# Running sums kept in PSUM, a shorter norm and casts moved to ScalarE, in an attention and two-MLP kernel

## Chip, cores and metric

The kernel runs on one core of a Trainium2 chip. The metric is the device time of one execution in microseconds (us). TensorE is called PE, VectorE DVE, ScalarE ACT, GpSimd POOL; SyncE (SP) issues the DMA transfers.

## The reference

```python
kv  = einsum('bhsd,bhse->bhde', k, v)          # linear attention, 8 batches x 8 heads, 576 x 64
out = einsum('bhsd,bhde->bhse', q, kv)
x   = out / sqrt(mean(out*out, -1) + 1e-6) * g_norm   # -> 4608 tokens x 512
h   = x @ w_in                                 # 512 -> 2048      (MLP one)
g   = maximum(h, 0) + log1p(exp(-abs(h)))      # softplus
x   = g @ w_out                                # 2048 -> 512
h   = maximum(maximum(x @ w1, x @ w2), x @ w3) # 512 -> 768       (MLP two)
y   = h @ w_out2                               # 768 -> 512
```

Everything is fp32, and all three projections of MLP one and two use the same tokens.

## The kernel before

The 4608 tokens are taken in five passes of 928, 928, 928, 928 and 896, each as two halves of N = 464 (448) columns. A matrix product over two halves of tokens and two halves of features is done by a scheme with seven block products instead of eight (`ORDER`: 1, 5, 6, 2, 7, 4, 3). One such set of seven is a *group*. The left factors are sums of weight blocks, the right factors sums of token blocks (`combine`). Pass 0 multiplies in plain fp32 and meanwhile converts the weights from 8-byte words (`to_f32`, `sums_of_weights`), splits each into a high and a low part (`make_unit`) and stores them to DRAM. Passes 1 to 4 load these units (`u`) and replace a product by three (high x high, high x low, low x high: `mm3`, lines 123 to 125). `split` makes the parts of a token block: a cast gives `hi` (line 107 on ACT, line 109 on DVE), then a subtraction gives `lo` (line 113, on POOL or DVE).

A pass has 16 groups for MLP one (H0 to H7 from x to h, X00 to X31 from g back to x), 9 groups for MLP two (three feature blocks f, and j = 0, 1, 2 for w1, w2, w3), and the output products. All work is written as events with a due time in *slots*; one slot is one product, a group begins every 7 slots, and groups overlap: `SLOT` puts a group's products at 0, 1, 3, 4, 6, 9, 12 slots after its beginning. Events are sorted by due time, and a scheduler that goes by its own estimates of durations fixes each engine's order when the kernel is built, so the order on an engine can differ from the written one.

The products accumulate in PSUM banks by tag: X (2 buffers; products 1, 6, 7, 4), Y (2; products 5, 3), W (1; product 2), `at` (2; attention and parts of the output), `cv` (1). `sums` takes the four result blocks out: C11 = X + W, C12 = X + Y, C22 = X + Y, C21 = X. ACT copies X to an SBUF tile, DVE adds the other bank to that tile, and the tile goes to `done`. For H groups `done` is `softplus`: ACT takes Abs, Exp and Ln (lines 346 to 348), DVE max(h, 0) + e (line 349). For MLP two it is the running maximum (line 617), and after j = 2 a split into `hh` and `hl`. W is also the bank of a temporary, t2, in `combine`.

`attention_beside` puts the next pass's attention into MLP two: eight head steps (two halves by four pairs of heads), 6 slots apart. A step at slot t loads q at t - 6, splits it at t - 3 (`split_q`: cast on DVE, low part on POOL), multiplies with kv at t + 0.3 (`out_mm`), squares and splits at t + 0.4 (`square`: Square on ACT, cast sh on DVE, low part sl on POOL, og = o * g on ACT), sums the squares with two matmuls against ones at t + 3.3 (`ssq_mm`, lines 465 and 466) and normalises at t + 3.4 (`norm`). `combine_x` takes the results at the end of the pass. All units u, the q and the k and v tiles are loaded by the one queue of SP.

At the border from X31 to MLP two, `combine_x2(q)` splits the two feature halves q = 0, 1 of x; the first group of MLP two cannot finish product 1 before the parts of q = 1 are there.

Of the kernel before, what the change touches and what calls it, by code (L numbers as in the profile page):

```python
# [7 lines left out]
F32 = mybir.dt.float32  # L8
# [7 lines left out]
P = 128  # L16
# [21 lines left out]
def kernel(  # L38
# [57 lines left out]
    gcol = const.tile([P, 1], F32, name="gcol")  # L96
    ones = const.tile([P, P], F32R, name="ones")
# [109 lines left out]
    def convert(g, i):  # L207
        if i == 0:
            sw[g] = pools["raw"].tile([P, 8, 256], F32, tag="sw", bufs=3, name="sw")
        w = sw[g]  # L210
        if i == 0:
            dst = w[:, PLACE[1]:PLACE[2] + 1:PLACE[2] - PLACE[1]]
        else:
            dst = w[:, PLACE[4]:8:7 - PLACE[4]]
        to_f32(raws.pop((g, i)), dst)

    def sums_of_weights(g):
        w = sw[g]
        a11, s1, s2, a12, s3, a22, s4 = (w[:, PLACE[m]] for m in (1, 5, 6, 2, 7, 4, 3))
        a21 = w[:, 7]  # L220
        add(nc.gpsimd, s1, a21, a22)
        sub(nc.gpsimd, s2, s1, a11)
        sub(nc.gpsimd, s3, a11, a21)
        sub(nc.gpsimd, s4, a12, s2)
# [31 lines left out]
    def combine(tile, dst, c, tiles, steps, t2_bank):  # L256


        b11, b12, b21, b22 = tiles
        n = b11.shape[1]  # L260
        for s in steps:
            for m in STEPS[s]:
                hi, lo = tile("hi", n, F32R), tile("lo", n, F32R)
                src = {1: b11, 2: b21, 3: b22, 7: b12, 4: b11}.get(m)
                if m == 5:
                    src = t1 = psum("cv", "t1")[:, 0:n]
                    sub(nc.vector, t1, b12, b11)
                elif m == 6:
                    src = t2 = psum(t2_bank, "t2")[:, 0:n]
                    sub(nc.vector, t2, b22, t1)  # L270
                    sub(nc.gpsimd, b12, b22, b12)
                    sub(nc.vector, b11, b21, t2)
                split(nc.scalar, src, hi, lo, nc.vector if m in (5, 6) else nc.gpsimd)
                dst[m, c] = (hi, lo)
# [42 lines left out]
    def sums(done, make):  # L317

        c = {}

        def after(m, b):
            if m == 1:
                c[11] = make(11)
                nc.scalar.copy(c[11], b["X"])
            elif m == 6:
                c[12] = make(12)
                nc.scalar.copy(c[12], b["X"])  # L327
            elif m == 2:
                add(nc.vector, c[11], c[11], b["W"])
                done(11, c[11])  # L330
            elif m == 7:
                c[22] = make(22)
                nc.scalar.copy(c[22], b["X"])
                add(nc.vector, c[22], c[22], b["Y"])
                done(22, c[22])
            elif m == 4:
                done(21, b["X"])
            elif m == 3:
                add(nc.vector, c[12], c[12], b["Y"])
                done(12, c[12])  # L340

        return after
# [73 lines left out]
    def split_q(a, n, p):  # L416
        q = q_t.pop((a, p))
        qh, ql = ctile("qh", n, F32R), ctile("ql", n, F32R)
        split(nc.vector, q, qh, ql, nc.gpsimd)
        qs[a, p] = (qh, ql)  # L420
# [30 lines left out]
    def square(a, n, p):  # L451
# [4 lines left out]
        split(nc.vector, sq, sh, sl, nc.gpsimd)  # L456
# [12 lines left out]
    def norm(a, n, p):  # L469

        ss = ss_t.pop((a, p))
        m, r, t = ctile("m", n), ctile("r", n), ctile("t", n)
        nc.vector.tensor_scalar(
            out=m, in0=ss, scalar1=1.0 / D, scalar2=EPS, op0=ALU.mult, op1=ALU.add
        )
        nc.scalar.activation(r, m, AF.Ln)
        nc.scalar.activation(r, r, AF.Exp, scale=-0.5)
        nc.scalar.activation(t, r, AF.Square)
        nc.vector.scalar_tensor_tensor(
            out=t, in0=t, scalar=-0.5, in1=m, op0=ALU.mult, op1=ALU.mult  # L480
        )
        nc.vector.scalar_tensor_tensor(  # L482
            out=r, in0=t, scalar=1.5, in1=r, op0=ALU.add, op1=ALU.mult
# [22 lines left out]
    def attention_beside(pas, t_kv, t0):  # L506
# [11 lines left out]
        for k in range(2 * NP):  # L518
# [7 lines left out]
            at(t + 3.3, ssq_mm, a, n, p)  # L526
            at(t + 3.4, norm, a, n, p)

    def run_pass(pas, base):
# [31 lines left out]
        for fp in range(8):  # L561
            t = start[f"H{fp}"]
            weights_at(t, G_H[fp])
            run_group(t, pas, G_H[fp], R,
                      sums(lambda w, src, fp=fp: h_done(fp, w, src), lambda w: ctile(f"h{w}", N)))
# [30 lines left out]
        def combine_x2(q):  # L596
            tiles = [x2[q, w] for w in TILES]
            if pas == 0:
                combine32(xc_tile, R2, q, tiles)
            else:  # L600
                combine(xc_tile, R2, q, tiles, ALL, "W")
# [26 lines left out]
        for k in range(9):  # L628
# [5 lines left out]
                           lambda w, j=j: ge_tile(pas, f"m{w}", N) if j == 0 else ctile(f"m{w}", N)))  # L634
# [61 lines left out]
    for j in range(2):  # L696
        r = slice(j * D, (j + 1) * D)
        nc.gpsimd.memset(ones[r, r].bitcast(F32), 1.0)
        nc.gpsimd.memset(ones32[r, r], 1.0)
    nc.sync.dma_start(out=gcol, in_=gn)  # L700

# [44 lines left out]
def _laid_out(inputs):  # L746
# [15 lines left out]
    def swapped(w):  # L762

        w = w.reshape(-1, 2, P, 2, DM // 2)
        w = np.stack([w[:, 0], w[:, 1, :, ::-1]], axis=1)
        return np.ascontiguousarray(w).reshape(-1, P, DM)

# [13 lines left out]
        "w_in": swapped(cols(inputs["moe_w_in"])),  # L781
        "w_out": swapped(wo.reshape(NF, P, DM)),
        "w123": np.ascontiguousarray(
            np.stack([swapped(cols(inputs[f"moe2_w{j}"])) for j in (1, 2, 3)], axis=1)
# [28 lines left out]
```

## Time and profile before

| | before |
|---|---|
| median of 3 runs (range) | 1546.93 us (1544.9 to 1549.52) |
| profiled execution: time, span | 1547.21 us, 1545.3 us |
| mean granted PE clock | 0.981 |
| busy share of span: PE, DVE, ACT, POOL | 94%, 63%, 52%, 50% |
| busy us: PE, DVE, ACT, POOL | 1447.1, 976.7, 805.7, 778.9 |
| DMA moved, mean rate | 315.58 MB, 204 GB/s |

The span runs from the first to the last instruction. Pass 0 ends at about 440 us; each later pass takes about 275 us. A row of a windows view gives, after the window, its length and then for PE, PE's weight loads, DVE, ACT and POOL the busy us with the number of instructions in brackets, then the granted PE clock as a share of full speed, the DMA share and GB/s. In a timeline a row gives start, length, engine, line, operation, output<-inputs, and in square brackets the idle time of the engine just before and what ended it.

### The profile page before, as it was taken

To read this page: it belongs to the slowest core of one execution; us is meant where nothing else is said; L and a number is where in the kernel's file an instruction comes from. 1 tells how busy PE (TensorE), PEld (TensorE's weight loads), DVE (VectorE), ACT (ScalarE), POOL (GpSimd) and SP (SyncE) were. 2 spreads that over 40 slices of the span, in tenths; PEclk is the share of its full clock that TensorE was granted. 3 is DMA by queue.
4 is the path that set the end of the run, shared out by engine and by line. 5 is a ranking of instruction groups with operands and counts; after the bars stand their busy time and mean duration, and the time that the engine had idled before them with its cause. 6 is when DMAs were issued, how large, how long until landed. Compare 5 with 4: busy or idle time off the path is not lost.

```text
span 1545.3 us, 18956 instructions
## 1 busy us (share of the span) xinstructions
PE 1447.1 (94%) x6164; PEld 1136.4 (74%) x6164; DVE 976.7 (63%) x1495; ACT 805.7 (52%) x1573; POOL 778.9 (50%) x692
## 2 busy tenths in 40 slices
PE   6699999888999998999999899999998999999898
PEld 4244444444478887888888788888887889898798
DVE  6687897768836665771766566456765753667332
ACT  4486552545448653553866344377635445774321
POOL 4668676867606444552435544534446551534311
PEclk9799999999999999999999999999999999999999
DMA  7547668665566676655567675566665656666563
GB/s 258 213 162 249 223 223 292 229 231 175 201 209 195 202 246 188 201 178 185 190 204 217 215 241 180 162 207 194 222 207 171 195 181 189 202 211 214 176 213 115
DMA packets 106803, 315.58 MB, mean 204 GB/s; under 512 B 11984, under 2 KB 22224, under 8 KB 106704
## 3 DMA queue, kind: packets, MB, share of 16 engines
q1 hardware_dynamic: 106704, 314.36, 62.2%
q8 instruction: 50, 0.82, 0.2%
q14 instruction: 49, 0.40, 0.1%
HBM read 255.85 MB, written 58.46 MB: 203 GB/s over the span
## 4 chain that ended last, share of the span: by engine, by line
PE 60%; ACT 12%; DVE 11%; POOL 8%; issue 4%; DMA 4%; SPq 0%; POOLq 0%; ACTq 0%; DVEq 0%
PE Xo L124 3%; PE Xo L125 3%; PE Xo L123 3%; PE Xx L123 3%; PE Xx L124 3%; PE Xx L125 3%; PE Xh L123 3%; PE Xh L125 3%; PE Xh L124 3%; DMA v<-in_vp_dram 2%; PE oacc L652 2%; PE oacc L124 2%; PE oacc L125 2%; PE oacc L123 2%; ACT hi L107 2%
## 5 line engine op out<-in xcount | busy, mean ns | idle before, releaser
L113 POOL TENSOR_TENSOR lo<-e,hi 128x464 fp32r<-128x464 f32 (+1 forms) x160 | 195.9, 1257 | 223.6 <-ACT hi L107 220.0
L349 DVE SCALAR_TENSOR_TENSOR e<-h,e 128x464 f32<-128x464 f32 (+1 forms) x120 | 113.8, 949 | 75.7 <-ACT e L348 75.4
L119 POOL TENSOR_TENSOR e<-e 128x464 f32<-128x464 f32 (+1 forms) x40 | 48.4, 1209 | 161.2 <-DVE t L119 147.0
L113 POOL TENSOR_TENSOR u<-sw,u 128x512 fp32r<-128x512 f32 (+1 forms) x100 | 119.5, 1221 | 11.5 <-ACT u L107 11.5
L124 PE MATMUL Xo<-lo,u 128*128 128x464 f32 (+1 forms) x288 | 109.4, 380 | 12.5 <-POOL lo L113 12.5
L123 PE MATMUL Xo<-hi,u 128*128 128x464 f32 (+1 forms) x288 | 108.3, 381 | 6.9 <-DMA u<-wd 5.6
L125 PE MATMUL Xo<-hi,u 128*128 128x464 f32 (+1 forms) x288 | 108.1, 378 | 0.0
L113 POOL TENSOR_TENSOR hl<-m,hh 128x464 fp32r<-128x464 f32 (+1 forms) x48 | 59.7, 1249 | 93.0 <-ACT hh L107 88.3
L346 ACT ACTIVATE e<-h 128x464 f32<-128x464 f32 (+1 forms) x120 | 70.3, 586 | 62.0 <-DVE h L116 62.0
L107 ACT CAST hi<-t 128x464 fp32r<-128x464 f32 (+1 forms) x96 | 52.2, 544 | 96.3 <-DVE t L119 39.4
L116 DVE TENSOR_TENSOR x<-x,Xx 128x464 f32<-128x464 f32 (+1 forms) x120 | 75.5, 629 | 41.5 <-PE Xx L125 34.2
L123 PE MATMUL Xh<-hi,u 128*128 128x464 f32 (+1 forms) x256 | 96.7, 378 | 3.7 <-ACT h L327 2.1
L123 PE MATMUL Xx<-hi,u 128*128 128x464 f32 (+1 forms) x256 | 95.5, 373 | 1.9 <-ACT x L582 1.9
L125 PE MATMUL Xx<-hi,u 128*128 128x464 f32 (+1 forms) x256 | 95.0, 371 | 0.0
L125 PE MATMUL Xh<-hi,u 128*128 128x464 f32 (+1 forms) x256 | 94.9, 371 | 0.0
L124 PE MATMUL Xx<-lo,u 128*128 128x464 f32 (+1 forms) x256 | 94.8, 370 | 0.0
L124 PE MATMUL Xh<-lo,u 128*128 128x464 f32 (+1 forms) x256 | 94.6, 370 | 0.0
L107 ACT CAST hi<-e 128x464 fp32r<-128x464 f32 (+1 forms) x160 | 87.4, 574 | 13.0 <-PE Yx L124 7.1
L347 ACT ACTIVATE e<-e 128x464 f32<-128x464 f32 (+1 forms) x160 | 92.7, 588 | 2.2
L348 ACT ACTIVATE e<-e 128x464 f32<-128x464 f32 (+1 forms) x160 | 92.5, 586 | 2.4
L486 POOL TENSOR_TENSOR og<-og,r 128x464 f32<-128x464 f32 (+1 forms) x40 | 52.2, 1306 | 64.7 <-DVE r L482 64.7
L187 ACT ACTIVATE cv<-raw 128x512 f32<-128x512 f32 x56 | 35.9, 640 | 85.0 <-DVE sw L198 44.5
(180 smaller groups left out, 4147.2 us busy)
## 6 DMA issues: line engine op xcount, KB each, us to landing
u<-wd SPq DMA_DIRECT2D x316, 512.0 KB, 4.2
wd<-u SPq DMA_DIRECT2D x79, 512.0 KB, 2.9
u<-wd SPq DMA_DIRECT2D x116, 256.0 KB, 3.7
raw<-in_w_out_dram SPq DMA_DIRECT2D x22, 512.0 KB, 4.3
k<-in_kp_dram SPq DMA_DIRECT2D x32, 320.0 KB, 4.1
v<-in_vp_dram SPq DMA_DIRECT2D x32, 320.0 KB, 4.4
raw<-in_w_dram SPq DMA_DIRECT2D x18, 512.0 KB, 3.6
raw<-in_w_in_dram SPq DMA_DIRECT2D x16, 512.0 KB, 4.2
```

Source lines behind the costliest of these rows:

```text
L107: nc.scalar.copy(hi, src)
L113: eng_lo.tensor_tensor(out=lo, in0=src, in1=hi.bitcast(F32), op=ALU.subtract)
L116: eng.tensor_tensor(out=o, in0=a, in1=b, op=ALU.add)
L119: eng.tensor_tensor(out=o, in0=a, in1=b, op=ALU.subtract)
L123: nc.tensor.matmul(acc, wh, xh, start=first, stop=False, skip_group_check=on)
L124: nc.tensor.matmul(acc, wh, xl, start=False, stop=False, skip_group_check=on)
L125: nc.tensor.matmul(acc, wl, xh, start=False, stop=last, skip_group_check=on)
L346: nc.scalar.activation(e, src, AF.Abs)
L347: nc.scalar.activation(e, e, AF.Exp, scale=-1.0)
L348: nc.scalar.activation(e, e, AF.Ln, bias=1.0)
L349: nc.vector.scalar_tensor_tensor(out=e, in0=src, scalar=0.0, in1=e, op0=ALU.max, op1=ALU.add)
L486: nc.gpsimd.tensor_tensor(out=og, in0=og, in1=r, op=ALU.mult)
```

## The change

- `sums`: C11 of every H group is added in place in bank W and not in the SBUF tile; softplus reads it there. In MLP two with j = 1, 2, C11 and C12 are added in place in W and Y and the maximum reads them there.
- `split_q` and `square`: the casts qh and sh go from DVE to ACT.
- `norm`: the tile m = ss/64 + eps and its DVE instruction are gone. Ln reads ss from PSUM with scale 1/64 and a bias column; the correction step reads ss from PSUM too, and g_norm is multiplied by -0.5 once at the start to make up for the other constants.
- `ssq_mm` and `norm` of each head step are due 1.5 slots later.
- `combine_x2(1)`: the low parts for products 1 and 2 are made on DVE and not on POOL.
- The weight block a21 lies in the place of sum s1, which is then formed in place: the `sw` tile has seven columns of blocks and not eight, s3 is formed ahead of s1, and the host no longer swaps blocks.

```diff
--- before.py
+++ after.py
@@ -94,6 +94,7 @@
         return gc_tile(name, n) if p == 0 else wide(pools["ge"], "ge", 17, name, n)
 
     gcol = const.tile([P, 1], F32, name="gcol")
+    epsc = const.tile([P, 1], F32, name="epsc")
     ones = const.tile([P, P], F32R, name="ones")
     ones32 = const.tile([P, P], F32, name="ones32")
     kvs = []
@@ -206,21 +207,20 @@
 
     def convert(g, i):
         if i == 0:
-            sw[g] = pools["raw"].tile([P, 8, 256], F32, tag="sw", bufs=3, name="sw")
+            sw[g] = pools["raw"].tile([P, 7, 256], F32, tag="sw", bufs=3, name="sw")
         w = sw[g]
         if i == 0:
             dst = w[:, PLACE[1]:PLACE[2] + 1:PLACE[2] - PLACE[1]]
         else:
-            dst = w[:, PLACE[4]:8:7 - PLACE[4]]
+            dst = w[:, PLACE[5]:PLACE[4] + 1:PLACE[4] - PLACE[5]]
         to_f32(raws.pop((g, i)), dst)
 
     def sums_of_weights(g):
         w = sw[g]
         a11, s1, s2, a12, s3, a22, s4 = (w[:, PLACE[m]] for m in (1, 5, 6, 2, 7, 4, 3))
-        a21 = w[:, 7]
-        add(nc.gpsimd, s1, a21, a22)
+        sub(nc.gpsimd, s3, a11, s1)
+        add(nc.gpsimd, s1, s1, a22)
         sub(nc.gpsimd, s2, s1, a11)
-        sub(nc.gpsimd, s3, a11, a21)
         sub(nc.gpsimd, s4, a12, s2)
 
     def make_unit(g, k):
@@ -253,7 +253,7 @@
     STEPS = ((1,), (5, 6), (2,), (7,), (4,), (3,))
     ALL = (0, 1, 2, 3, 4, 5)
 
-    def combine(tile, dst, c, tiles, steps, t2_bank):
+    def combine(tile, dst, c, tiles, steps, t2_bank, on_dve=()):
 
 
         b11, b12, b21, b22 = tiles
@@ -270,7 +270,7 @@
                     sub(nc.vector, t2, b22, t1)
                     sub(nc.gpsimd, b12, b22, b12)
                     sub(nc.vector, b11, b21, t2)
-                split(nc.scalar, src, hi, lo, nc.vector if m in (5, 6) else nc.gpsimd)
+                split(nc.scalar, src, hi, lo, nc.vector if m in (5, 6, *on_dve) else nc.gpsimd)
                 dst[m, c] = (hi, lo)
 
     def combine32(tile, dst, c, tiles):
@@ -316,28 +316,33 @@
 
     def sums(done, make):
 
+
         c = {}
+
+        def total(w, bank):
+            tile, kept = c.pop(w)
+            to = tile if kept else bank
+            add(nc.vector, to, tile, bank)
+            done(w, to)
+
+        def copy(w, b):
+            c[w] = make(w)
+            nc.scalar.copy(c[w][0], b["X"])
 
         def after(m, b):
             if m == 1:
-                c[11] = make(11)
-                nc.scalar.copy(c[11], b["X"])
+                copy(11, b)
             elif m == 6:
-                c[12] = make(12)
-                nc.scalar.copy(c[12], b["X"])
+                copy(12, b)
             elif m == 2:
-                add(nc.vector, c[11], c[11], b["W"])
-                done(11, c[11])
+                total(11, b["W"])
             elif m == 7:
-                c[22] = make(22)
-                nc.scalar.copy(c[22], b["X"])
-                add(nc.vector, c[22], c[22], b["Y"])
-                done(22, c[22])
+                copy(22, b)
+                total(22, b["Y"])
             elif m == 4:
                 done(21, b["X"])
             elif m == 3:
-                add(nc.vector, c[12], c[12], b["Y"])
-                done(12, c[12])
+                total(12, b["Y"])
 
         return after
 
@@ -416,7 +421,7 @@
     def split_q(a, n, p):
         q = q_t.pop((a, p))
         qh, ql = ctile("qh", n, F32R), ctile("ql", n, F32R)
-        split(nc.vector, q, qh, ql, nc.gpsimd)
+        split(nc.scalar, q, qh, ql, nc.gpsimd)
         qs[a, p] = (qh, ql)
 
     def out_mm32(a, n, p, tag):
@@ -453,7 +458,7 @@
         sq = ctile("sq", n)
         sh, sl = ctile("sh", n, F32R), ctile("sl", n, F32R)
         nc.scalar.activation(sq, o, AF.Square)
-        split(nc.vector, sq, sh, sl, nc.gpsimd)
+        split(nc.scalar, sq, sh, sl, nc.gpsimd)
         og = xr_tile(1, "og", n)
         nc.scalar.mul(og, o, gcol)
         sq_t[a, p] = (sh, sl)
@@ -469,18 +474,15 @@
     def norm(a, n, p):
 
         ss = ss_t.pop((a, p))
-        m, r, t = ctile("m", n), ctile("r", n), ctile("t", n)
-        nc.vector.tensor_scalar(
-            out=m, in0=ss, scalar1=1.0 / D, scalar2=EPS, op0=ALU.mult, op1=ALU.add
-        )
-        nc.scalar.activation(r, m, AF.Ln)
+        r, t = ctile("r", n), ctile("t", n)
+        nc.scalar.activation(r, ss, AF.Ln, scale=1.0 / D, bias=epsc)
         nc.scalar.activation(r, r, AF.Exp, scale=-0.5)
-        nc.scalar.activation(t, r, AF.Square)
+        nc.scalar.activation(t, r, AF.Square, scale=0.125)
         nc.vector.scalar_tensor_tensor(
-            out=t, in0=t, scalar=-0.5, in1=m, op0=ALU.mult, op1=ALU.mult
+            out=t, in0=ss, scalar=D * EPS, in1=t, op0=ALU.add, op1=ALU.mult
         )
         nc.vector.scalar_tensor_tensor(
-            out=r, in0=t, scalar=1.5, in1=r, op0=ALU.add, op1=ALU.mult
+            out=r, in0=t, scalar=-3.0, in1=r, op0=ALU.add, op1=ALU.mult
         )
         og = og_t[a, p]
         nc.gpsimd.tensor_tensor(out=og, in0=og, in1=r, op=ALU.mult)
@@ -523,8 +525,8 @@
             at(t - 3, split_q, a, n, p)
             at(t + 0.3, out_mm, a, n, p)
             at(t + 0.4, square, a, n, p)
-            at(t + 3.3, ssq_mm, a, n, p)
-            at(t + 3.4, norm, a, n, p)
+            at(t + 4.8, ssq_mm, a, n, p)
+            at(t + 4.9, norm, a, n, p)
 
     def run_pass(pas, base):
 
@@ -562,7 +564,7 @@
             t = start[f"H{fp}"]
             weights_at(t, G_H[fp])
             run_group(t, pas, G_H[fp], R,
-                      sums(lambda w, src, fp=fp: h_done(fp, w, src), lambda w: ctile(f"h{w}", N)))
+                      sums(lambda w, src, fp=fp: h_done(fp, w, src), lambda w: (ctile(f"h{w}", N), w != 11)))
         for n in range(4):
             gc[n] = {}
             if n == 0 or pas == 0:
@@ -598,7 +600,7 @@
             if pas == 0:
                 combine32(xc_tile, R2, q, tiles)
             else:
-                combine(xc_tile, R2, q, tiles, ALL, "W")
+                combine(xc_tile, R2, q, tiles, ALL, "W", (1, 2) if q else ())
 
         for q in range(2):
             at(start[f"X3{q}"] + 12.5, combine_x2, q)
@@ -631,7 +633,8 @@
             weights_at(t, G_2[fp][j])
             run_group(t, pas, G_2[fp][j], R2,
                       sums(lambda w, src, fp=fp, j=j: h2_done(fp, j, w, src),
-                           lambda w, j=j: ge_tile(pas, f"m{w}", N) if j == 0 else ctile(f"m{w}", N)))
+                           lambda w, j=j: ((ge_tile(pas, f"m{w}", N), True) if j == 0
+                                          else (ctile(f"m{w}", N), w == 22))))
         base3 = base2 + 63
         if pas + 1 < NPASS:
             attention_beside(pas + 1, start["X30"], base2)
@@ -697,7 +700,9 @@
         r = slice(j * D, (j + 1) * D)
         nc.gpsimd.memset(ones[r, r].bitcast(F32), 1.0)
         nc.gpsimd.memset(ones32[r, r], 1.0)
+    nc.gpsimd.memset(epsc, EPS)
     nc.sync.dma_start(out=gcol, in_=gn)
+    nc.vector.tensor_scalar(out=gcol, in0=gcol, scalar1=-0.5, scalar2=None, op0=ALU.mult)
 
 
     t = -60
...
```

## Rows read from the trace of the kernel before

**Rows 1.** Busy time in 20 us windows from 440 us on, granted clock, DMA

```profile
540.00:560.00 20.00, 20.00 (x97) 17.87 (x96) 14.72 (x23) 13.48 (x25) 6.51 (x5) 1.00 0.69 220
...
580.00:600.00 20.00, 15.33 (x73) 13.04 (x72) 10.70 (x18) 4.93 (x10) 8.38 (x7) 1.00 0.52 163
...
660.00:680.00 20.00, 17.96 (x77) 15.34 (x77) 12.90 (x19) 10.93 (x21) 11.05 (x10) 0.91 0.49 157
...
1420.00:1440.00 20.00, 14.72 (x63) 12.51 (x62) 10.80 (x18) 5.11 (x11) 8.13 (x7) 0.91 0.45 133
...
sum 1100.00, PE 1059.17 PEld 940.09 DVE 647.41 ACT 586.51 POOL 485.62; mean PE 19.26 PEld 17.09 DVE 11.77 ACT 10.66 POOL 8.83
```

**Rows 2.** The same in 10 us windows, 0 to 450 us (pass 0)

```profile
290.00:300.00 10.00, 7.67 (x16) 3.40 (x15) 7.25 (x14) 6.57 (x13) 8.40 (x10) 0.83 0.39 133
...
350.00:360.00 10.00, 6.92 (x18) 3.52 (x18) 7.88 (x11) 3.98 (x8) 8.97 (x10) 0.87 0.63 221
...
sum 450.00, PE 396.64 PEld 204.29 DVE 330.71 ACT 224.42 POOL 293.75; mean PE 8.81 PEld 4.54 DVE 7.35 ACT 4.99 POOL 6.53
```

**Rows 3.** Waits of PE, whole span: total us, times, longest us

```profile
PE ss L466 <- POOL sl L113: 13.4, 8, 3.1
...
PE Xo L124 <- POOL lo L113: 12.5, 4, 3.6
...
PE Xo L123 <- DMA u<-wd: 5.6, 3, 2.2
...
PE ss L465 <- DVE sh L109: 3.3, 4, 1.0
```

**Rows 4.** Waits of PE, 70 to 440 us only

```profile
PE ss L466 <- POOL sl L113: 8.2, 5, 3.1
```

**Rows 5.** Timeline around one ssq_mm: start us, length us, engine, line

```profile
661.59 0.39 DVE L109 CAST sh<-sq 128x464 fp32r<-128x464 f32 x1
...
661.75 1.26 POOL L486 TENSOR_TENSOR og<-og,r 128x464 f32<-128x464 f32 x1 [0.58 <-DVE r L482]
...
662.97 1.16 POOL L113 TENSOR_TENSOR sl<-sq,sh 128x464 fp32r<-128x464 f32 x1
...
664.18 0.48 PE L466 MATMUL ss<-sl,ones 128*128 128x464 f32 x1 [1.67 <-POOL sl L113]
```

**Rows 6.** Timeline where X31 ends and MLP two begins, pass 1

```profile
590.09 2.50 ACT L107 CAST hi<-x 128x464 fp32r<-128x464 f32 x5
...
590.75 3.85 POOL L113 TENSOR_TENSOR lo<-x,hi 128x464 fp32r<-128x464 f32 x3 [2.78 <-ACT hi L107]
...
591.68 0.74 DVE L119 TENSOR_TENSOR t<-x,x 128x464 f32<-128x464 f32 x1
...
595.68 2.27 POOL L113 TENSOR_TENSOR lo<-x,hi 128x464 fp32r<-128x464 f32 x2
...
598.01 0.48 PE L124 MATMUL Xo<-lo,u 128*128 128x464 f32 x1 [3.35 <-POOL lo L113]
```

**Rows 7.** Instruction groups, shapes apart: count, busy us, mean ns, idle before

```profile
L349 DVE SCALAR_TENSOR_TENSOR e<-h,e 128x464 f32<-128x464 f32 x96 | 90.0, 937 | 58.4 <-ACT e L348 58.1
...
L349 DVE SCALAR_TENSOR_TENSOR e<-Xh,e 128x464 f32<-128x464 f32 x32 | 20.3, 634 | 10.4 <-ACT e L348 10.3
...
L109 DVE CAST qh<-qraw 128x464 fp32r<-128x464 f32 x24 | 20.2, 843 | 1.8 <-DMA qraw<-in_qt_dram 1.6
...
L473 DVE TENSOR_SCALAR m<-ss 128x464 f32<-128x464 f32 x32 | 20.3, 634 | 6.5 <-PE ss L466 4.6 <-PE ss L440 1.8
...
L107 ACT CAST hi<-x 128x464 fp32r<-128x464 f32 x30 | 15.9, 581 | 12.1 <-DVE x L116 12.1
```

**Rows 8.** Timeline of bank W, H3 to X00 in pass 1

```profile
469.89 0.62 DVE L116 TENSOR_TENSOR h<-h,Wh 128x464 f32<-128x464 f32 x1
...
472.57 0.45 PE L123 MATMUL Wx<-hi,u 128*128 128x464 f32 x1 [0.90 <-DVE e L119]
...
475.81 1.47 DVE L349 SCALAR_TENSOR_TENSOR e<-h,e 128x464 f32<-128x464 f32 x1 [1.08 <-ACT e L348]
```

More of the change, by code (lines that the diff above doesn't have):

```diff
@@ L760, in cols @@
         return np.ascontiguousarray(w.reshape(KC, P, n, P).transpose(2, 1, 0, 3)).reshape(n, P, KC * P)
[L762 to L766, printed above, removed]
     wo = inputs["moe_w_out"].reshape(4, 2, 2, P, 2, 2, P).transpose(0, 5, 4, 3, 2, 1, 6)
@@ L780, in _laid_out @@
         "gn": np.tile(inputs["g_norm"], 2).reshape(P, 1),
-        "w_in": swapped(cols(inputs["moe_w_in"])),
-        "w_out": swapped(wo.reshape(NF, P, DM)),
+        "w_in": cols(inputs["moe_w_in"]),
+        "w_out": np.ascontiguousarray(wo).reshape(NF, P, DM),
         "w123": np.ascontiguousarray(
-            np.stack([swapped(cols(inputs[f"moe2_w{j}"])) for j in (1, 2, 3)], axis=1)
+            np.stack([cols(inputs[f"moe2_w{j}"]) for j in (1, 2, 3)], axis=1)
         ),
```

## The prediction

> **What bounds the kernel now.** I read the windows view first, in 20 us steps behind pass 0 and 10 us steps inside it. From 440 us on PE is busy for 1059 of 1100 us, while DVE has 647, ACT 587 and POOL 486 [rows 1]. A full window, such as 540 to 560, holds 97 PE instructions, so one matmul is issued every 20 / 97 = 0.206 us and a slot (six matmuls) is 1.24 us. PE sets the end, and time saved on another engine counts only where PE waits for that engine. The 41 us in which PE stands are bunched: 580 to 600, where X31 hands over to MLP two, lacks 4.7 us; 660 to 680 lacks 2.0 us; 1420 to 1440, the border of pass 4, lacks 5.3 us. In the last two the granted clock is 0.91 too: part of the window ran at 1.2 instead of 2.4 GHz after PE had stood, which costs 20 x 0.09 = 1.8 us on top. Pass 0 is looser: PE 397 of 450 us, DVE 331, with stretches at a clock of 0.83 and 0.87 [rows 2].
>
> Second, the view of waits, for PE alone, says who ended these gaps [rows 3]. The second matmul of `ssq_mm` waits for sl from POOL: 13.4 us in 8 waits, the longest 3.1; the first waits for sh from DVE, 3.3 us. Product 1 of the first group of MLP two waits for a low part from POOL, 12.5 us in 4 waits, one per pass from 1 to 4. The transfer of a unit costs 5.6 us. In pass 0 the wait for sl has 8.2 of its 13.4 us [rows 4], which leaves 5.2 for passes 1 to 3. The 3.3 us for sh I count with passes 1 to 3.
>
> **The squares.** The timeline shows how such a wait arises [rows 5]: sh is ready at 661.98, but POOL does og of the step before until 663.0 and only then sl, until 664.13; PE takes up its matmul at 664.18 after 1.67 us. The change makes `ssq_mm` due 1.5 slots = 1.9 us later. The mean of the 8 waits is 13.4 / 8 = 1.7 us, so most vanish, and of the longest 3.1 some 1.2 stay. The norm moves by as much, so og of the step before should now fall behind sl. The cast sh on ACT costs 0.58 us by the like cast hi<-x [rows 7], against 0.39 on DVE in this step [rows 5]; ACT has the room.
>
> With the waits go clock dips. One window like 660 to 680 stands in each of passes 1 to 3: 3 x 1.8 = 5.4 us. In pass 0 the windows at 290 and 350 us lost 1.7 and 1.3 us to the clock [rows 2], together 3.0. So passes 1 to 3 hold 5.2 + 3.3 + 5.4 = 13.9 us, pass 0 8.2 + 3.0 = 11.2. I take four fifths of the first, 11.1, since part of the longest waits stays. Of the second I take two thirds, 7.5, since in pass 0 a PE that is early may stand at the weight conversion instead.
>
> What is late next: the norm ends later, and `combine_x` waits for og. The last norm is due 54.9 slots after MLP two begins, the first step that needs its og at 64.5, so 9.6 slots = 11.9 us. The chain is three ACT instructions, two on DVE and one on POOL. At 0.58, 0.634 and 1.26 us [rows 7, 5] that is 4.3 us. It is hidden, and even if 1.9 us more came of it. The removed instruction for m (0.634 us) shortens it.
>
> **The border.** At 590 us ACT casts five hi in 2.50 us; POOL makes three low parts by 594.60, a difference of 1.15 us, two more low parts from 595.68, and PE gets the part for q = 1 only at 598.01, after 3.35 us [rows 6]. The queue on POOL is what PE waits for, since the part's hi is cast by 592.59. On DVE a low part costs about 0.63 us as other DVE subtractions do (t<-x,x took 0.74 in this very place [rows 6]), so it is ready at some 593.4, before PE stood (598.01 - 3.35 = 594.66). That removes the 12.5 us of four borders and the 1.8 us of clock in pass 4: 14.3. Behind the two subtractions on DVE stand t1 and t2 and the low parts of products 5 and 6; each is 0.63 to 1.3 us later. I take four fifths, 11.4. The 5.6 us of unit transfers I leave.
>
> **Sums in PSUM.** The last softplus instruction costs 937 ns with both inputs in SBUF and 634 with one in PSUM [rows 7], so 0.30 us less for each C11; I take the same for the maximum. The Trainium skill, in "SBUF — State Buffer", section Who interferes with whom, says that a DVE instruction with two SBUF inputs contends with a GpSimd instruction that reads SBUF, and that the second to start blocks fully. The two means agree with it. By that rule the low parts moved to DVE, with both inputs in SBUF, are the kind that blocks, while POOL is busy beside them; what it would do is the second rival.
>
> For pass 0 the relief of DVE per head step is 0.843 (qh), 0.39 to 0.84 (sh) and 0.634 (m): 1.9 to 2.3 us, over 8 steps 15 to 18; with 20 x 0.30 = 6 us for 8 sums and 12 maxima, 21 to 24 us of 331. If only as much of it reaches PE as PE's idle share, 53 / 450, it is worth 24 x 0.12 = 2.8 us; it could be nothing, or at most 24. I take 2, near the low end because the rows name POOL and not DVE as what PE waits for. In the other passes PE hides it.
>
> The cost lies in holding banks. Bank W has one buffer. In the last H group before X00, the add into C11 ran at 469.89 and the last softplus instruction at 475.81, yet PE began the next product in W at 472.57 [rows 8]. Now W is free at 475.81 + 0.63 = 476.44 at the earliest, 3.9 us later than PE used it. PE can put other products first if the order allows; if it cannot, such a place costs 3.9 + 1.8 (clock) = 5.7 us. Likewise ss stays in its `at` buffer for four instructions, 3 x 0.58 + 0.63 = 2.4 us, and not 0.63; the next ss comes 6 slots = 7.4 us later. Bounds: 0, and 8 places (two tight ones in each of passes 1 to 4) x 5.7 = 46. I take 3, half a place: near the low end, since X and Y offer other work.
>
> The weight sums are the same four POOL instructions in another order, s1 one instruction later; the split that follows on POOL waits for all four, which hides it. One extra DVE instruction at the start is nothing beside 1500 us. The bias column of Ln is priced at nothing; ACT's room covers it.
>
> **The sum.** - 7.5 - 11.1 - 11.4 - 2 + 3 = - 29.0 us. The profiled execution took 1547.2 us (its span 1545.3), 0.3 above the median 1546.9, so the two can be used alike: 1547.2 - 29.0 = 1518.
>
> **Rivals.**
> *The wait for sl moves along.* POOL orders sl, og and the q parts anew, and `ssq_mm` finds sl late again. For it: POOL is the engine that is late in 8 of 12 waits. Against it: the move is longer than the mean wait, and POOL has 50% free. The gains of 7.5 and 11.1 fail: 1537. Chance 0.14.
> *The border keeps its gap.* The low parts on DVE are blocked by POOL's, up to one POOL instruction (3.85 / 3 = 1.28 us) for each of the four DVE instructions in a row there, 5.1 us, which is more than the 3.35 that PE waited; or product 6 becomes the one that is late. Against it: t<-x,x took 0.74 us beside a busy POOL [rows 6]. The 11.4 us fail: 1530. Chance 0.11. The rule of the skill named above is this blocking.
> *Both fail:* about 1548, within 0.3% of before. Chance 0.06.
> *Bank W holds PE up, and the kernel is slower.* ACT is nearly full while H0 to H3 run in a row, softplus of C11 slips behind other work, and product 2 of the next group finds W taken. Price 5.7 us a place; with the other gains kept (1547.2 - 32 = 1515) it turns slower from the sixth place on; with all 8 it is 1515 + 46 = 1561. For it: the times in rows 8. Against it: only the groups with no X group between them are that tight. Chance 0.11.
>
> **How the numbers follow.** My forecast has 0.58, with a range of its own from 1506 to 1533 (all shares in full to half of them). The low end takes 13.9 + 11.2 + 14.3 in full, the 5.6 of the transfers and 2.8 for DVE: 48, so 1499. The high end of 1543 takes in the first two rivals and leaves out the equal and the slower case, 0.17. Faster by over 0.3% (4.6 us, about what a measurement can tell): 0.58 + 0.14 + 0.11 = 0.83; within 0.3%: 0.06; slower: 0.11.
>
> **What would show it.** Right: in the waits of PE, ss for sl falls from 13.4 to under 4 us, Xo for lo from 12.5 to under 3; the 20 us window behind each border has over 18 us of PE; the windows at 0.91 are gone; the group m<-ss is absent. Wrong: PE waits for W after a softplus instruction; ss still waits for POOL; a new wait for the parts of product 6 at the border; or pass 0 still ends at 440 us though its waits for sl are gone.

## The result, and the profile after

The changed kernel takes 1503.12 us (median of 4 runs, 1501.59 to 1504.92) against 1548.22 for the kernel before beside it: ratio 0.9705, 95% interval [0.9673, 0.9737], 45 us faster. The forecast was 1518. The profiled execution took 1502.64 us, its span 1500.8.

The page's busy times: PE still fills the span, and DVE lost 95 us of work.

```profile
PE 1424.8 (95%) x6164; PEld 1129.3 (75%) x6164; DVE 881.6 (59%) x1400; ACT 836.2 (56%) x1637; POOL 752.6 (50%) x685
```

The waits of PE after the change, over the whole span (total us, times, longest). They answer to [rows 3]:

```profile
PE Xo L124 <- DMA u<-wd: 6.7, 4, 2.2
...
PE Xh L124 <- ACT h L330: 5.2, 8, 0.9
PE Xh L297 <- DVE t L120: 5.1, 1, 5.1
...
PE ss L471 <- POOL sl L114: 4.3, 2, 3.5
...
PE Xo L125 <- DVE lo L114: 0.8, 4, 0.2
```

The wait for sl fell from 13.4 to 4.3 us, that for the low part at the border from 12.5 to 0.8; the transfer u (6.7) is now the first thing that PE waits for at the border. No line names bank W. The first low part of the border on DVE shows how [rows 6] changed, in the timeline of the same place of pass 1:

```profile
576.33 2.50 ACT L108 CAST hi<-x 128x464 fp32r<-128x464 f32 x5
...
576.99 4.27 POOL L114 TENSOR_TENSOR lo<-x,hi 128x464 fp32r<-128x464 f32 x3 [2.76 <-ACT hi L108]
...
578.86 1.34 DVE L114 TENSOR_TENSOR lo<-x,hi 128x464 fp32r<-128x464 f32 x1 [0.18 <-ACT hi L108]
...
579.05 0.45 PE L124 MATMUL Xo<-hi,u 128*128 128x464 f32 x1 [1.38 <-DMA u<-wd]
...
581.45 0.37 PE L125 MATMUL Xo<-lo,u 128*128 128x464 f32 x1
```

DVE ends its part at 580.20 while POOL is still at its three (until 581.26), and the next product into Xo with a low part starts without standing. A wait of 0.2 us for DVE is left at each border (0.8 in all). In 20 us windows at the borders of passes 1, 2 and 4 (against [rows 1]) PE has 18.3, 18.3 and 17.5 us, at full clock; one window at 0.91 is left, with 18.1 us of PE, at the border of pass 3:

```profile
560.00:580.00 20.00, 18.33 (x93) 16.24 (x93) 13.65 (x22) 6.30 (x13) 7.73 (x7) 1.00 0.75 253
...
840.00:860.00 20.00, 18.27 (x86) 15.50 (x86) 13.49 (x21) 9.96 (x20) 12.43 (x10) 1.00 0.61 188
...
1120.00:1140.00 20.00, 18.12 (x80) 15.62 (x79) 12.49 (x21) 9.91 (x20) 11.29 (x10) 0.91 0.55 172
1380.00:1400.00 20.00, 17.48 (x83) 14.89 (x82) 13.27 (x22) 8.25 (x17) 10.99 (x10) 1.00 0.62 188
```

A ruler for all that follows: the start of the first product into Xh of each pass, read in PE's timeline, cuts the span into pass 0 and passes 1 to 4 (the last ends with the span). "Standing" is the length of passes 1 to 4 less PE's busy time there, by the windows view (its end cut at the full microsecond). Each row's passes and standing come from one profiled execution, the median from all runs; single executions of one kernel lie several us apart. The kernel before ran again in each job, with medians from 1547.9 to 1550.1 us. The last columns are the measured median and its ratio to the kernel before in the same job.

| kernel | pass 0, us | passes 1 to 4 | standing there | median | ratio [95%] |
|---|---|---|---|---|---|
| before | 438.9 | 1106.4 | 44.5 | 1548.22 | 1 |
| changed | 425.6 | 1075.2 | 22.3 | 1503.12 | 0.9705 [0.9673, 0.9737] |
| border alone (a_border) | 440.0 | 1093.8 | 32.5 | 1535.93 | 0.9899 [0.9865, 0.9934] |
| later squares alone (a_late) | 442.7 | 1106.8 | 41.9 | 1550.05 | 0.9994 [0.9976, 1.0013] |
| norm alone (a_norm) | 424.8 | 1098.6 | 36.9 | 1525.36 | 0.9847 [0.9821, 0.9873] |
| casts alone (a_casts) | 437.7 | 1104.4 | 41.7 | 1541.86 | 0.9949 [0.9933, 0.9966] |
| PSUM sums alone (psum) | 435.3 | 1097.1 | 39.0 | 1533.77 | 0.9918 [0.9890, 0.9946] |
| mean on ACT (mact) | 432.9 | 1105.3 | 43.4 | 1542.69 | 0.9957 [0.9941, 0.9974] |
| border, norm, casts (combo) | 419.5 | 1080.9 | 25.7 | 1507.05 | 0.9735 [0.9710, 0.9760] |

The gain of 44.5 us between the two profiled spans is 13.3 in pass 0 and 31.2 behind it.

### The profile page after: what moved, and what is told of

Same layout as the page of the kernel before. It is cut to its first block, busy times and chain, and to the rows that moved or that the text cites. A ratio compares the mean times of both kernels' runs of the same rounds, so it can differ in the third digit from the quotient of the medians.

```text
span 1500.8 us, 18903 instructions
## 1 busy us (share of the span) xinstructions
PE 1424.8 (95%) x6164; PEld 1129.3 (75%) x6164; DVE 881.6 (59%) x1400; ACT 836.2 (56%) x1637; POOL 752.6 (50%) x685
## 4 chain that ended last, share of the span: by engine, by line
PE 70%; ACT 8%; DVE 7%; DMA 6%; POOL 5%; issue 3%; SPq 0%; POOLq 0%; ACTq 0%; DVEq 0%
PE Xo L125 4%; PE Xo L124 4%; PE Xo L126 4%; PE Xx L124 3%; PE Xx L125 3%; PE Xx L126 3%; PE Xh L124 3%; DMA v<-in_vp_dram 3%; PE Xh L126 3%; PE Xh L125 3%; PE oacc L124 3%; PE oacc L126 3%; PE oacc L125 3%; PE oacc L655 2%; PE Yo L124 2%
## 5 line engine op out<-in xcount | busy, mean ns | idle before, releaser
L114 POOL TENSOR_TENSOR lo<-e,hi 128x464 fp32r<-128x464 f32 (+1 forms) x160 | 190.6, 1225 | 233.8 <-ACT hi L108 233.8
L114 POOL TENSOR_TENSOR u<-sw,u 128x512 fp32r<-128x512 f32 (+1 forms) x100 | 115.7, 1185 | 10.3 <-ACT u L108 10.3
L330 ACT COPY m<-Xo 128x464 f32<-128x464 f32 (+1 forms) x135 | 72.8, 542 | 78.5 <-PE Xo L126 73.2
L354 DVE SCALAR_TENSOR_TENSOR e<-h,e 128x464 f32<-128x464 f32 (+1 forms) x80 | 70.6, 882 | 49.0 <-ACT e L353 48.9
L108 ACT CAST hi<-e 128x464 fp32r<-128x464 f32 (+1 forms) x160 | 87.8, 577 | 12.6 <-PE Yx L125 7.0
L330 ACT COPY h<-Xh 128x464 f32<-128x464 f32 (+1 forms) x120 | 63.7, 536 | 47.7 <-PE Xh L126 34.8
```

Of the source, the lines that this page charges most:

```text
L108: nc.scalar.copy(hi, src)
L114: eng_lo.tensor_tensor(out=lo, in0=src, in1=hi.bitcast(F32), op=ALU.subtract)
L330: nc.scalar.copy(c[w][0], b["X"])
L354: nc.vector.scalar_tensor_tensor(out=e, in0=src, scalar=0.0, in1=e, op0=ALU.max, op1=ALU.add)
```

## The experiments

The first four do one part alone, to see which terms of the sum hold.

**The border.**

```diff
-    def combine(tile, dst, c, tiles, steps, t2_bank):
+    def combine(tile, dst, c, tiles, steps, t2_bank, on_dve=()):
...
-                split(nc.scalar, src, hi, lo, nc.vector if m in (5, 6) else nc.gpsimd)
+                split(nc.scalar, src, hi, lo, nc.vector if m in (5, 6, *on_dve) else nc.gpsimd)
...
-                combine(xc_tile, R2, q, tiles, ALL, "W")
+                combine(xc_tile, R2, q, tiles, ALL, "W", (1, 2) if q else ())
```

> The kernel before with one part alone: low parts of products 1 and 2 of q = 1 at the border on DVE. Theory A (PE's waits are what the parts remove, and they add up): the 12.5 us of waits for the low part go but for under 1 us, with the 1.8 us of clock in pass 4, so 1.3 to 1.5 us x 10, that is -13 to -15 us, about 1534; pass 0 and the squares unchanged. Theory B (every build draws a new order on all engines, and the gain belongs to the order and not to a part): the gain is not at the borders, or is far from 14.

It took 1535.93 us; 1 - 0.9899 of 1550 is 16 us. In the profile passes 1 to 4 are 12.6 us shorter and pass 0 is not. The wait for lo from POOL (12.5 us) is gone, 0.8 us for lo from DVE are left, and PE stands 12.0 us less behind pass 0. So the gain lies at the borders, against theory B, and the term holds.

**The later squares.**

```diff
-            at(t + 3.3, ssq_mm, a, n, p)
-            at(t + 3.4, norm, a, n, p)
+            at(t + 4.8, ssq_mm, a, n, p)
+            at(t + 4.9, norm, a, n, p)
```

> The kernel before with one part alone: ssq_mm and norm 1.5 slots later. Theory A: passes 1 to 3 lose the waits for sl and sh (5.2 + 2.3) and the clock dips (5.4), -12 to -14 us; pass 0 -4 to -11; together -17 to -24, about 1526. Theory B: less than 10, because POOL is ordered anew and sl is late in other places. Theory C (sl is late because DVE casts and POOL block each other, so the later place needs the casts on ACT to work): waits for sl fall by less than half.

Nothing: 1550.05 us, 0.9994. The waits of this run show what became of the term of 18.6 us:

```profile
PE Xo L124 <- POOL lo L113: 10.8, 4, 3.4
PE ss L466 <- POOL sl L113: 9.6, 6, 2.3
PE Xo L297 <- ACT m L327: 6.4, 5, 1.6
```

Only 3.8 of the 13.4 us for sl went, 3.4 of them in pass 0, and a wait for ACT's copy m, 1.4 us before, took 6.4, all of it in pass 0. Behind pass 0 the wait for sl stayed (5.2 to 4.8 us); PE stood 2.6 us less, but its busy time for the same matmuls grew by 2.8 (1061.6 to 1064.4). That fits theory B. That the later place needs the casts on ACT (theory C) is tested by b_nolate below.

**The norm without its mean tile.**

```diff
-        nc.vector.tensor_scalar(
-            out=m, in0=ss, scalar1=1.0 / D, scalar2=EPS, op0=ALU.mult, op1=ALU.add
-        )
-        nc.scalar.activation(r, m, AF.Ln)
+        nc.scalar.activation(r, ss, AF.Ln, scale=1.0 / D, bias=epsc)
...
```

The correction step and the constants change with it, as in the whole change.

> The kernel before with one part alone: the norm without its mean tile. Theory A: PE waits for the norm only before the first groups of pass 0 (og and t), so 0 to -3 us, 1545 to 1547. Theory D (the 8 us that the changed kernel is ahead when the first X group of pass 0 begins come from the shorter norm chain and its reordering of the start): -6 to -10 us, all of it before 115 us.

The largest part, 24 us, a miss for both theories; the prediction had priced the removed instruction at a share of its 2 us for the relief of DVE. Pass 0 ends 14.1 us earlier, 9.9 of them by the first product into Xx (97.1 us, 107.0 before), so theory D has the place of a part and not the size. Passes 1 to 4 are 7.8 us shorter, and the wait for sl is still 10.7 us in 7 waits.

**The casts on ACT.**

```diff
-        split(nc.vector, q, qh, ql, nc.gpsimd)
+        split(nc.scalar, q, qh, ql, nc.gpsimd)
...
-        split(nc.vector, sq, sh, sl, nc.gpsimd)
+        split(nc.scalar, sq, sh, sl, nc.gpsimd)
```

> The kernel before with one part alone: casts of q and of the squares on ACT. Theory A: only PE's waits for sh (3.3 us) go, 0 to -4 us, about 1545. Theory E (DVE is the limit of pass 0 in its MLP two, and 2 x 0.8 us less of it per head step is worth its time there): -6 to -13 us, all between 250 and 400 us.

8 us faster by the medians, though the wait for sl grew:

```profile
PE ss L466 <- POOL sl L113: 15.7, 12, 4.4
```

So this wait is not a price: it grows by 2.3 us in a kernel that is 8 us faster. All of the growth is in pass 0 (8.2 to 12.7 us; behind it 5.2 fell to 3.0), and pass 0 still ends 1.2 us earlier. The size is the one of theory E, its place is not shown: the profiled execution has 1.2 us in pass 0 and 2.0 behind it.

Two readings of the norm's gain were open. Theory F: the tile m occupied one of the ten buffers of its tag (the tiles of `ctile`), and a free buffer lets other work start earlier. Theory G: the chain of the norm became shorter by one trip from PE through DVE to ACT, in DVE's ordered queue. Theory H asked in addition whether the later squares need such a buffer to pay. Three kernels change the number of buffers ("c", 10) and one undoes the later squares in the changed kernel.

```diff
-        return wide(cp, "c", 10, name, n, dtype)
+        return wide(cp, "c", 11, name, n, dtype)
```

> The kernel before with 11 buffers in the pool of the tiles q, sq, m, r, t, h and out (tag c) and not 10, nothing else. Theory F (buffers: the norm alone gave 24 us because without the tile m a head step at the start of pass 0 holds 4 of the 10 buffers and not 5, so 2.5 and not 2 steps are under way and q is loaded every 4.5 and not every 6 us): 11 / 5 = 2.2 steps, so some 40% of the way, 6 to 12 us, most of it before the first X group of pass 0. Theory G (the shorter chain: the instruction for m and its wait): 0, within 3 us of before.

1546.99 us, 0.9994 [0.9976, 1.0011]: one more buffer is worth nothing.

The norm alone with 8 buffers instead of 10 (the same line with 8):

> The norm without its mean tile alone, but with 8 buffers in that pool and not 10: 8 / 4 = 2 steps under way, as before with 10 / 5. Theory F: the gain of 24 us is gone, 1545 or slower, and q is loaded every 6 us at the start again. Theory G: the gain stays, under 1530.

1528.79 us, 0.9867 [0.9850, 0.9883]. With two buffers fewer the gain stays, so F falls.

The later squares with 11 buffers:

> ssq_mm and norm 1.5 slots later, alone, with 11 buffers in that pool. Theory F: the later sums alone gave nothing because sq, sh and sl keep three of the ten buffers for 1.9 us longer and what they hold up eats the gain; with one more buffer the run is 8 us or more faster than the 11 buffers without the later sums. Theory H (the place of ssq_mm is worth nothing, since POOL is ordered anew and sl is late again): within 4 us of the 11 buffers alone.

1546.73 us, 0.9979 [0.9967, 0.9991]: at most 5 us against the kernel before, and by the medians within 1 us of the 11 buffers alone, as theory H says.

The changed kernel with `ssq_mm` and `norm` back at t + 3.3 and t + 3.4:

> The changed kernel with ssq_mm and norm back in their old places (3.3 and 3.4 slots), the rest as changed. Theory F: with the tile m gone there are buffers, the later place is worth its waits and dips in passes 1 to 3, so it is slower than the changed kernel by 8 to 15 us, 1511 to 1518, and the waits of PE for sl return. Theory H: within 4 us of 1503.

1505.0 us, 0.9706 [0.9692, 0.9721], where the changed kernel has 0.9705. Its PE waits 9.9 us for sl in 8 waits, 5.6 more than in the changed kernel. The later place is worth nothing in either kernel, with the casts on DVE or on ACT, so theory C falls too.

The last four run theory G against its parts and ask whether the parts add.

**The mean on ACT.** m keeps its tile and its instruction:

```diff
-        nc.vector.tensor_scalar(
-            out=m, in0=ss, scalar1=1.0 / D, scalar2=EPS, op0=ALU.mult, op1=ALU.add
-        )
+        nc.scalar.activation(m, ss, AF.Identity, scale=1.0 / D, bias=epsc)
...
```

> The kernel before, with one edit: the mean over the 64 rows (m = ss/64 + eps) is still written to its own tile by an instruction of its own, but on ACT instead of DVE. Theory G1, the trip into DVE's ordered queue is what costs: 12 to 24 us faster than before (1525 to 1537), the eight head steps at the start of pass 0 some 4.5 to 5 us apart instead of 6.3. Theory G2, the instruction and its tile cost wherever they run: within 4 us of before. A result between 4 and 12 us would give a part to each.

1542.69 us, 0.9957 [0.9941, 0.9974]: 7 us faster, a part to each. Pass 0 ends 6.0 us earlier (14.1 without the instruction); passes 1 to 4 gain 1.1 (7.8 without it). DVE is relieved of the same 40 instructions, 25 us, in both kernels, so its relief, with the work put on ACT, brings these 7 us; the rest needs the step gone.

**Three parts together**, the edits of a_border, a_norm and a_casts:

> The kernel before with three parts only: the border (first low parts of MLP two on DVE before the split's loop), the norm without its mean tile, and the two casts on ACT. The sum of squares stays at its old places, and sums C11 and C12 go as before. If the parts add: -15 - 24 - 8 = -47, so about 1502, as the whole change. If the PSUM sums or the later squares carry a part of the whole gain, it stays above 1510.

1507.05 us: 41 us of the 45. That lies between the two outcomes that were expected (1502 and over 1510) and decides for neither; the intervals of combo and of the changed kernel overlap, so the 4 us between them are not clear of noise. In the profile these three give 19.4 us in pass 0 and 25.5 behind it, and its PE still waits 12.2 us for sl.

**The PSUM sums alone.** `total` adds in place in the bank where the tile is not kept:

```diff
...
-                add(nc.vector, c[11], c[11], b["W"])
-                done(11, c[11])
+                total(11, b["W"])
...
+                      sums(lambda w, src, fp=fp: h_done(fp, w, src), lambda w: (ctile(f"h{w}", N), w != 11)))
...
```

> The kernel before with the sums C11 and C12 left in PSUM for softplus and maximum, nothing else changed. My theory: two DVE copies less in each pair, off the path, and no wait of TensorE for the bank: within 4 us of before. The rival of the prediction (the bank is held longer and TensorE waits for it): up to 46 us slower, with TensorE waiting on the tile of the fold's sums.

A miss for both sides: 1533.77 us, 13 us faster. (The expectation speaks of two DVE copies less; the profile has the same 1495 DVE instructions, and they are shorter.) PE waits nowhere for W: at the place of [rows 8] the bank comes free at 472.39, and PE, which does products into X and Y until then, takes it at 472.84 without standing.

```profile
471.75 0.64 DVE L353 SCALAR_TENSOR_TENSOR e<-Wh,e 128x464 f32<-128x464 f32 x1 [1.05 <-ACT e L352]
...
472.84 0.37 PE L123 MATMUL Wx<-hi,u 128*128 128x464 f32 x1
```

The instruction groups of this run (count, busy us, mean ns, idle before), and the maxima of the kernel before:

```profile
L353 DVE SCALAR_TENSOR_TENSOR e<-h,e 128x464 f32<-128x464 f32 x64 | 56.4, 881 | 34.8 <-ACT e L352 34.5
...
L353 DVE SCALAR_TENSOR_TENSOR e<-Wh,e 128x464 f32<-128x464 f32 x32 | 20.5, 641 | 25.4 <-ACT e L352 25.3
...
L621 DVE TENSOR_TENSOR m<-m,Wo 128x464 f32<-128x464 f32 x24 | 15.2, 632 | 0.5
```

```profile
L617 DVE TENSOR_TENSOR m<-m,m 128x464 f32<-128x464 f32 x72 | 62.2, 863 | 0.9
```

One third of the 96 softplus ends [rows 7] dropped from a mean of 937 to 641 ns, and the maxima with a bank as input take 632, where the kernel before had 72 of 863 ns with both inputs in SBUF. DVE is busy 33 us less (976.7 to 943.6) and POOL 16 us less (778.9 to 762.7), for the same instructions.

**One more visit to DVE removed.** In the changed kernel og = o * g of pass 0 (the expectation calls it a square) goes to ACT:

```diff
-        nc.vector.tensor_scalar(out=og_t[a, p], in0=o, scalar1=gcol, scalar2=None, op0=ALU.mult)
+        nc.scalar.mul(og_t[a, p], o, gcol)
```

> The changed kernel, with the first square of the output head's norm in pass 0 (og) on ACT instead of DVE, one visit less to DVE's ordered queue. Theory G: 2 to 6 us faster than the changed kernel (1497 to 1501). Rival: at that place ACT is as long in coming as DVE, so within 2 us of it (1501 to 1505).

1502.49 us, 0.9709 [0.9685, 0.9733], against 0.9705: nothing, and the rival holds. This og stands beside the chain (it needs the product o and not the sum of squares), so theory G in the plain form "one DVE instruction fewer helps" is too wide. Its profiled execution is the longest of its four (1506.40 us, the others 1499.42 to 1504.60): the eighth sum of squares starts there at 55.91 us and not at 48.99 as in the changed kernel, and pass 0 ends 3.4 us later. A few us between two single profiles are thus not the worth of a part.

## Why the prediction was right and wrong

**What bounds the kernel: right.** PE's instructions are the same 6164, and the gain is PE standing less and waiting less at the lower clock. Behind pass 0 the standing fell from 44.5 to 22.3 us; the other 9 of the 31.2 us are PE's busy time for the same matmuls (1061.6 to 1052.1 us), as when fewer of them run at the lower clock.

**The squares, -7.5 and -11.1: failed.** The step that failed is "The change makes `ssq_mm` due 1.5 slots = 1.9 us later ... so most vanish", and with it the step from a wait to its price. The places are worth nothing, alone (0.9994) or undone (0.9706 against 0.9705). The wait for sl did fall in the changed kernel, but the wait in the view was no price: b_nolate waits 9.9 us for sl, the changed kernel 4.3, and the two are equal in time. I had read how long PE stood at one instruction, and not whether what follows would have stood anyway. The readings were off by a little too: of the 3.3 us for sh, 1.0 lies in pass 0, and the window at 0.91 that I counted for pass 3 (1160 to 1180) holds the wait of 3.6 us for lo at that pass's border, and no head step's wait.

**The norm: the mis-sized part.** The step that failed is "It is hidden ... The removed instruction for m (0.634 us) shortens it". I looked at the deadline of the last norm in passes 1 to 4, and not at the start of pass 0, where PE has to wait for what the eight head steps deliver. The first of them in the kernel before, in the timeline:

```profile
15.13 1.91 PE L440 MATMUL ss<-sq,ones 128*128 128x464 f32 x2 [0.65 <-ACT sq L434]
17.08 0.64 DVE L473 TENSOR_SCALAR m<-ss 128x464 f32<-128x464 f32 x1 [1.27 <-PE ss L440]
17.76 0.59 ACT L476 ACTIVATE r<-m 128x464 f32<-128x464 f32 x1 [2.68 <-DVE m L473]
...
21.25 0.64 DVE L479 SCALAR_TENSOR_TENSOR t<-t,m 128x464 f32<-128x464 f32 x1
...
21.50 1.05 PE L440 MATMUL ss<-sq,ones 128*128 128x464 f32 x2 [0.24 <-ACT sq L434]
22.43 1.38 DVE L482 SCALAR_TENSOR_TENSOR r<-t,r 128x464 f32<-128x464 f32 x1
```

and with the norm alone changed:

```profile
14.54 1.05 PE L441 MATMUL ss<-sq,ones 128*128 128x464 f32 x2 [0.65 <-ACT sq L435]
...
15.62 0.65 ACT L474 ACTIVATE r<-ss,epsc 128x464 f32<-128x464 f32 x1 [1.14 <-PE ss L441]
...
18.44 0.64 DVE L477 SCALAR_TENSOR_TENSOR t<-ss,t 128x464 f32<-128x464 f32 x1
...
19.05 1.05 PE L441 MATMUL ss<-sq,ones 128*128 128x464 f32 x2 [1.57 <-ACT sq L435]
19.60 1.17 DVE L480 SCALAR_TENSOR_TENSOR r<-t,r 128x464 f32<-128x464 f32 x1
```

From the sum's start to the end of r the chain takes 8.7 us before (15.13 to 23.81) and 6.2 after (14.54 to 20.77), and the next step's ss starts 6.4 and 4.5 us behind this one. The eighth sum starts at 59.31 before and at 49.27 with the new norm. Not all of that is m itself: the two matmuls of the first row take 1.91 us in the one and 1.05 in the other, at a granted clock of 1.00 in both, and why they do no row tells. The next things that differ are a wait for og, which the norm delivers, and the clock. The longest such wait, before and with the norm alone changed:

```profile
44.57 1.91 PE L297 MATMUL Wh<-og,sw 128*128 128x464 f32 x2 [5.05 <-POOL og L486]
```

```profile
36.78 1.51 PE L298 MATMUL Wh<-og,sw 128*128 128x464 f32 x2 [2.49 <-POOL og L484]
```

Around and after it PE is granted a lower clock (windows of before, 40 to 60 us):

```profile
40.00:50.00 10.00, 4.78 (x8) 2.43 (x9) 4.66 (x8) 3.56 (x7) 5.94 (x6) 0.67 0.74 255
50.00:60.00 10.00, 7.83 (x17) 3.57 (x15) 8.18 (x13) 5.62 (x11) 5.57 (x7) 0.65 0.46 148
```

With the norm alone the same two windows have 0.97 and 0.89, and the one from 30 to 40 has 0.86 where the kernel before had 1.00. It is 10 us ahead at the eighth sum, 9.9 at the first product into Xx and 14.1 at the end of pass 0. Of the 9.9 us PE's standing makes 2.7 (26.6 to 23.9 us); the larger part is its busy time, 80.4 us for 231 matmuls before and 73.2 for 227 with the norm alone, at a mean granted clock of 0.90 and 0.96. Behind pass 0 PE stands 7.6 us less (44.5 to 36.9): the waits for sl fell from 5.2 to 1.9 us, those for sh from 2.3 to 0.7, those for e from 2.8 to 0.9.

With m on ACT the first sums come 4.3 to 6.3 us apart, but the eighth starts at 59.42 us, no earlier than before; at the first product into Xx that kernel is 3.5 us ahead (clock 0.93), at the end of pass 0 6.0. So the distance of the sums alone does not carry the gain. That the step gone from the chain pays is shown by the times (24 us without it, 7 with it on ACT). Which link of the chain brings which share, and what the new order of the engines adds, is not shown.

**The border, -11.4: right in place, a little small.** 12.6 us in passes 1 to 4 by the profile, 16 by the ratio of the runs. The low part took 1.34 us beside POOL and not 0.63 (mean of the six: 987 ns), as the rule of the Trainium skill in "SBUF — State Buffer", section Who interferes with whom, would have it for two SBUF inputs. But POOL's run of three lasts until 581.26 and DVE's part starts and ends inside it, so DVE was held for about 0.7 us and not for the run; the part came in time, and the rival "keeps its gap" falls. POOL is held as well: of its three (shortest, median, longest in ns, by the view of the tile lo) the first, from 576.99, takes 1.19 us, and the two during which DVE subtracts with two SBUF inputs take 1.59 each.

```profile
L114 POOL TENSOR_TENSOR lo<-x,hi x3: 1187/1587/1590, 577.0 to 579.7; 128x464 fp32r<-128x464 f32 x3
```

**Relief of DVE, -2, and bank W, +3: both mis-sized.** W: no wait, so 0 in place of +3; PE does put other products first, as I had allowed. Relief: the PSUM sums alone give 13 us (3.6 in pass 0, 9.3 behind it) and the casts 8, where I had scaled the relief by PE's idle share and left out the later passes ("PE hides it"). Of PE's small waits for DVE in passes 1 to 4, sh (2.3 us) and e (2.8 us) are gone with the PSUM sums, the wait for sl fell by 1.0, and the waits for ACT's h grew by 1.4. In all PE stands 5.5 us less (44.5 to 39.0) and is busy 3.9 us less for the same matmuls (1061.6 to 1057.7). That the shorter DVE and POOL instructions are what brings this is the likely reading; no run takes the one without the other.

**The sum.** The five single runs add to 3.9% or 61 us by their ratios (0.0101 + 0.0006 + 0.0153 + 0.0051 + 0.0082), against 2.95%, 45 us, for the whole, so by the medians the parts overlap by some 16 us. By the single profiled spans they add to 45.3 us, against 44.5: there is no overlap, but a single execution can lie 5 us from its median (combo 1502.1 and 1507.1). Where the overlap is lost cannot be read from one profile of each.

Combo lacks only the later squares, the PSUM sums and the new layout of the weight sums. What it lacks gives about 4 us on top of it, not clear of noise, and not the 13 of the PSUM sums alone. In the two profiles the whole is 5.7 us ahead of combo behind pass 0 and 6.1 us behind in pass 0. Of the 6.1 us, 2.8 are there at the first product into Xx (98.9 and 96.1 us), 6.1 at the first into Xo (252.8 and 246.7). To the first part belongs a place where PE stood for 5.15 us for t at 64.64, which DVE could only make after og from POOL, in the window whose clock is 0.66; combo stood 1.35 us at the like place. The window from 60 to 70 us, first of the changed kernel, then of combo:

```profile
60.00:70.00 10.00, 5.36 (x9) 2.54 (x10) 2.23 (x2) 0.55 (x1) 6.74 (x6) 0.66 0.64 231
```

```profile
60.00:70.00 10.00, 8.65 (x22) 3.69 (x21) 3.39 (x6) 3.82 (x8) 6.48 (x6) 1.00 0.51 184
```

The two other kernels with PSUM sums and the new layout end pass 0 late too (b_nolate 429.8, after_og 429.0), three kernels with the new norm and without these two parts end it earlier on the whole (combo 419.5, a_norm 424.8, norm_c8 426.2), by one execution each. Whether the PSUM sums or the new layout (which acts on POOL, in pass 0) is the reason stays open: the layout was not run by itself, nor was combo with the PSUM sums.

**The rivals.** "The wait for sl moves along" did not happen in the changed kernel (4.3 us are left), though in a_late most of it stayed (9.6 of 13.4 us). Its outcome, that the gains of 7.5 and 11.1 fail, came true for another reason: as b_nolate shows, the wait costs nothing where it stays. "Bank W holds PE up" is refuted by psum. The forecast was 15 us too high: 18.6 us for the squares that were worth nothing, against 45 for norm, casts and PSUM sums, for which I had allowed -2 and +3; two errors of opposite sign. That the time came out inside the range of 1499 to 1543 is luck: 1503 lies below the forecast's own range of 1506 to 1533, and the low end got there by taking every gain in full, 25.1 us for the squares among them.

**The signs.** Of the signs named for "right", the wait for lo (0.8 us) and the group m<-ss, which is gone, came as said. The wait for sl fell to 4.3 us and not under 4, three of the four border windows have over 18 us of PE and the fourth 17.5, and one window at 0.91 is left. Of the signs for "wrong", PE does not wait for W and pass 0 ends at 425.6 us and not at 440; ss still waits for POOL in two places (4.3 us), and the new wait at the border is there, but with 0.2 us each time: in pass 1 at 584.21, right after DVE ended a low part of t at 584.16.

## What to carry to other kernels

A wait in the list is where the engine stood, not what its removal is worth: do one part alone before pricing it, and expect the next wait in its place. Look for stretches where the bounding engine waits for one dependent chain (here the first 100 us); there a step of the chain counts several times, by the repeats and, in this case, by the lower clock that PE was granted there (a mean of 0.90, and 0.96 with the shorter chain). Reading a running sum from PSUM can shorten the instruction that follows and the ones on the neighbouring engine, so price it by the measured means of both forms. Do not take a few us between two profiles for the worth of a part.

## What the runs showed of the hardware

- The sum left in PSUM made POOL's unchanged instructions 16 us shorter in total and DVE's 33 us, in 692 and 1495 instructions. What the two engines cost each other is paid on both sides: at the border of pass 1 a DVE subtraction of two SBUF inputs took 1.34 us and not 0.63, and POOL's subtractions beside such ones 1.59 and not 1.19.
- A DVE cast of one SBUF input is not of one length: sh took 0.39 us in [rows 5], while its 24 instances of this shape average 756 ns and those of qh 843; all 32 of sh lie between 379 and 1415 ns. On ACT the same casts average 582 and 585 ns, and all 32 of sh lie between 561 and 590.
- PE's clock: in the changed kernel's window from 60 to 70 us 0.66 of full speed is granted, part of it thus at 1.2 GHz, and PE had stood for 5.15 us before 64.64; the two matmuls that follow took 1.92 us, and two like ones in combo at 62.83, at a clock of 1.00, took 1.05.
